# The convolution of a batch in other chunks between the pieces of a large matmul, and one copy moved ahead of the next stage

## Chip, cores, metric

One core of a Trainium2 chip (trn2). The metric is the device time of one execution in microseconds (us). Every run quoted gave a correct result. The profiled span is some 1.8 us shorter than the device time of the same execution.

## The reference, cut

```
# x: (8, 4224, 192) f32; weight: (8 heads, 7 taps)
w = softmax(weight, axis=-1)                       # per head
x = causal convolution over the sequence, 7 taps, head h on its 24 channels
h = x^T @ U @ V                                    # U (4224, 32), V (32, 4224): mixes the sequence
u = x + h^T
out = u + max(u @ w_ch1, 0) @ w_ch2                # 192 -> 768 -> 192
```

## The kernel before

It works in bf16 with float32 accumulation. A *group* is 8 tiles of 128 sequence positions, 33 groups in all. W1 is the product with `w_ch1` and its relu, W2 that with `w_ch2`. A late *stage* `k` does W1 of three groups and then twelve pieces of W2 (12 matmuls each); between the pieces it does the work that later stages need: the convolution of batch `k-2` (`c`), the collection `y^T U` (`t`), its sum (`s`), and the low-rank product and addition (`h`). The number ahead of the colon is the piece ahead of which it is done.

```
elif k < 10:                      # stages of batches 4 to 7 (k = 6 to 9)
    b = k - 2
    at = {
        1: [f"c{b}:0:3:AAD"],     # first head : heads : engines that evict (A ScalarE, D VectorE)
        2: [f"c{b}:3:3:AAD"],
        3: [f"c{b}:6:2:A"] + ([f"x{b + 1}:3"] if b + 1 < B else []),
        5: [f"t{b}", hs[0]],
        7: [f"s{b}"],
        8: [hs[1]],
        11: [hs[2]],
    }
```

Matmuls write into eight *banks* of PSUM, taken in rotation. An *eviction* is the operation by which ScalarE or VectorE brings a result out of its bank; only when it is over can the bank be taken again.

The convolution reads x and a copy of it shifted across partitions, `xb`. GpSimd makes that copy in six steps. `x5:3` runs three of them at that place in the program; the others follow one by one behind the loads of the next x, which matmuls of the next W1 let go:

```
def conv32(b, h0, nh, engs):
    ...
    for n in range(nh):
        pp = [bank(), bank()]                     # 8 PSUM banks, in rotation
        for cg in range(4):                       # 64x32 tiles: x and xb by turns
            ...
        for part in range(2):
            evac(engs[(2 * n + part) % len(engs)], yt[b][...], pp[part][...])
...
for g in gs1:
    ends = w1(g, ...)
    for b, blocks in LOADS.items():
        for q, (gb, m) in enumerate(blocks):
            if gb == g:
                x_load(b, q, ends[m])             # held back until that matmul of W1
                if steps:
                    steps.pop(0)()                # one copy of xb
```

`xb` has one buffer, so the copies for the next batch can start only when the convolution of this one is over. The evictions of W1 are alternately ScalarE's and VectorE's (seven and five of twelve a group).

## Time and profile before

| | before |
|---|---|
| three runs ahead of the prediction, median (range) | 325.4 us (325.24 to 325.87) |
| profiled span | 323.5 us |
| TensorE busy, granted clock | 317.1 us (98%), 1.00 |
| VectorE, ScalarE, GpSimd busy | 269.1, 170.4, 142.7 us |
| W1 to next W1, stages of batches 4 to 7 | 28.04, 28.28, 28.13, 28.12 us (112.57 in all) |
| W1's end to the collection, in each of them | 7.19 to 7.20 us |

The last two rows are differences of start times in the chain of the work that ended last, whose columns are start (us), length (us), engine, tile, line and number of instructions. L554 is W1, L583 W2, L339 the convolution, L402 the collection, L428 the sum, L457 the low-rank product.

### The profile page before, as it was taken

The page shows a single profiled execution, that of the slowest core. Times are in us where ns is not written, and L with a number is a line of the kernel's source. Part 1 is how long each engine was busy: PE and PEld are TensorE (multiplying, and loading weights), DVE is VectorE, ACT ScalarE, POOL GpSimd, SP SyncE. Part 2 cuts the span into 40 slices and gives each one's busy share as a digit, 9 for nine tenths or more (in the row PEclk, how much of TensorE's full clock was granted, in tenths as well). Part 3 has the DMA queues.
Part 4 walks back from the last instruction along what each step waited for, and adds up shares of the span by engine and source line. Part 5 has one row for each costly group of instructions (what it writes and reads, how often), then busy time and mean ns, then how long its engine had stood idle before and what let it go on. Part 6 is the DMA issues. An engine that isn't in the chain of part 4 may idle for free.

```text
span 323.5 us, 9584 instructions
## 1 busy us (share of the span) xinstructions
PE 317.1 (98%) x3996; PEld 223.2 (69%) x3996; DVE 269.1 (83%) x551; ACT 170.4 (53%) x344; POOL 142.7 (44%) x111
## 2 busy tenths in 40 slices
PE   6999999999999999999999999999999999999996
PEld 3757676478677647866864784587797497487495
DVE  6769989987977986998798699879898897896864
ACT  1766624860874397088339708824903902912920
POOL 8664179729947694786859497000000000000000
PEclk9999999999999999999999999999999999999999
DMA  8999993999996899699699976139269059048035
GB/s 104 192 192 178 209 211 99 203 195 248 210 153 180 229 175 169 170 162 195 166 238 183 192 162 181 33 112 244 58 168 267 8 149 268 25 121 271 2 119 176
DMA packets 122907, 53.52 MB, mean 165 GB/s; under 512 B 87760, under 2 KB 122832, under 8 KB 122864
## 3 DMA queue, kind: packets, MB, share of 16 engines
q1 hardware_dynamic: 84528, 38.08, 47.0%
q0 software_dynamic: 38192, 14.73, 39.6%
q8 instruction: 31, 0.51, 0.7%
q14 instruction: 12, 0.10, 0.1%
q10 hardware_dynamic: 144, 0.10, 0.1%
HBM read 29.49 MB, written 25.95 MB: 171 GB/s over the span
## 4 chain that ended last, share of the span: by engine, by line
PE 92%; ACT 3%; DMA 2%; DVE 1%; issue 0%; POOL 0%; POOLq 0%
PE ps L583 42%; PE ps L554 39%; PE ps L339 3%; PE ps L457 3%; DMA x_sb<-in_x_dram 2%; PE ps L402 2%; ACT rl_sb L568 2%; PE ps L369 1%; ACT y_sb L256 1%; PE ps L509 1%; DVE u_sb L479 1%; DVE rl_sb L570 1%; PE ps L524 0%; PE ps L428 0%; POOL x_sb L79 0%
## 5 line engine op out<-in xcount | busy, mean ns | idle before, releaser
L568 ACT ACTIVATE rl_sb<-ps 128x512 bf16<-128x512 f32 x233 | 124.3, 603 | 108.0 <-PE ps L554 96.0
L583 PE MATMUL ps<-W_sb,rl_sb 128*128 128x192 bf16 x1584 | 141.9, 246 | 0.2
L583 PEld LDWEIGHTS <-rl_sb 128*128 128x128 bf16 x1584 | 128.1, 98 | 13.5 <-issue 13.1
L554 PE MATMUL ps<-uT,W_sb 64*128 64x512 bf16 x1188 | 131.7, 376 | 0.0
L570 DVE TENSOR_SCALAR rl_sb<-ps 128x512 bf16<-128x512 f32 x163 | 105.3, 688 | 15.7 <-PE ps L554 15.4
L554 PEld LDWEIGHTS <-W_sb 64*128 64x128 bf16 x1188 | 66.9, 94 | 60.5 <-issue 3.9
L592 DVE TENSOR_TENSOR out_sb<-ps,u_sb 128x384 f32<-128x384 f32 (+1 forms) x133 | 70.4, 550 | 25.9 <-PE ps L583 25.4
L305 POOL COPY xb_sb<-x_sb 32x3072 bf16<-32x3072 bf16 (+1 forms) x24 | 67.6, 2826 | 0.7
L479 DVE TENSOR_TENSOR u_sb<-y_sb,ps 128x192 bf16<-128x192 bf16 (+1 forms) x168 | 66.3, 461 | 0.0
L293 POOL COPY xb_sb<-x_sb 128x3072 bf16<-128x3072 bf16 x12 | 32.6, 2744 | 34.6 <-PE ps L339 25.7
L256 ACT ACTIVATE y_sb<-ps 128x384 bf16<-128x384 f32 (+4 forms) x90 | 38.2, 514 | 10.7 <-PE ps L339 7.9
L79 POOL DMA_DIRECT2D x_sb<-in_x_dram x32 | 27.1, 849 | 17.5 <-PE ps L554 10.5
L258 DVE CAST y_sb<-ps 128x408 bf16<-128x408 f32 (+4 forms) x36 | 19.2, 578 | 1.1 <-PE ps L369 0.9
L457 PE MATMUL ps<-tt_sb,V_sb 32*128 32x192 bf16 x264 | 12.4, 246 | 0.1
L339 PE MATMUL ps<-xb_sb,band 64*32 64x384 bf16 x192 | 12.1, 332 | 0.0
L339 PE MATMUL ps<-x_sb,band 64*32 64x384 bf16 x192 | 12.1, 333 | 0.0
L457 PEld LDWEIGHTS <-V_sb 32*128 32x128 bf16 x264 | 4.7, 92 | 7.3 <-issue 7.3
L416 ACT ACTIVATE tt_hi<-ps 128x192 bf16<-128x192 f32 x8 | 2.6, 331 | 10.9 <-PE ps L402 10.9
L369 PE MATMUL ps<-x_sb,band 64*64 64x240 bf16 (+3 forms) x192 | 8.1, 276 | 0.3 <-DMA x_sb<-in_x_dram 0.3
L369 PEld LDWEIGHTS <-band 64*64 64x64 bf16 x192 | 6.0, 106 | 2.2 <-issue 1.5
L339 PEld LDWEIGHTS <-band 64*32 64x32 bf16 x384 | 4.5, 89 | 4.1 <-issue 3.0
L402 PE MATMUL ps<-y_sb,U_sb 128*32 128x192 bf16 x258 | 7.4, 247 | 0.0
(65 smaller groups left out, 69.0 us busy)
## 6 DMA issues: line engine op xcount, KB each, us to landing
out_dram<-out_sb SPq DMA_DIRECT2D x131, 192.0 KB, 2.7
x_sb<-in_x_dram POOLq DMA_DIRECT2D x14, 384.0 KB, 7.3
x_sb<-in_x_dram POOLq DMA_DIRECT2D x7, 432.0 KB, 7.3
x_sb<-in_x_dram POOLq DMA_DIRECT2D x7, 408.0 KB, 8.0
x_sb<-in_x_dram POOLq DMA_DIRECT2D x1, 504.0 KB, 7.6
uT<-u_sb SPq DMA_TRANSPOSE x31, 3.9
x_sb<-in_x_dram POOLq DMA_DIRECT2D x1, 480.0 KB, 5.9
W_sb<-in_moe_w_ch_dram POOLq DMA_DIRECT2D x2, 192.0 KB, 7.6
```

The costliest lines, as they stand in the source:

```text
L79: return nc.gpsimd.dma_start(out=xt[b][HB * r : HB * r + HB, s0:s1, :], in_=x[b, blk * HB : (blk + s1 - s0) * HB, :].rearrange("(j p) d -> ...
L256: nc.scalar.activation(out=out, in_=in_, func=ACT.Copy)
L293: nc.gpsimd.tensor_copy(out=xbt[b][:, s0:s1, :], in_=xt[b][:, s0 + 1 : s1 + 1, :])
L305: nc.gpsimd.tensor_copy(out=xbt[b][q, s0:s1, :], in_=xt[b][q, s0:s1, :])
L339: nc.tensor.matmul(out=pp[r][QB * cg : QB * cg + QB, 0 : nk[r] * GS], lhsT=w[hr], rhs=t[hr, st : st + 2 * nk[r] - 1 : 2, hs], start=True, ...
L457: nc.tensor.matmul(out=banks[pr][:, a * D : (a + 1) * D], lhsT=V_sb[32 * q : 32 * q + 32, (j // 8) * 2 + j % 2, :], rhs=ttb[b][32 * q : 32 ...
L479: nc.vector.tensor_tensor(out=u_group(g)[:, i : i + n, :, hf, :], in0=yt[b][:, run[0] : run[0] + n, :].rearrange("p n (c k) -> p n c k", c=3),
L554: last = nc.tensor.matmul(out=pps[m][hf][:], lhsT=W1_sb[HB * hf : HB * hf + HB, c, m * P : (m + 1) * P], rhs=uTt[g][HB * hf : HB * hf + HB ...
L568: nc.scalar.activation(out=rl[:, m, hf, :], in_=pp[hf][:], func=ACT.Relu)
L570: nc.vector.tensor_scalar_max(out=rl[:, m, hf, :], in0=pp[hf][:], scalar1=0.0)
L583: last = nc.tensor.matmul(out=cps[:, a * D : (a + 1) * D], lhsT=rlt[g][:, m, hf, (i + a) * P : (i + a + 1) * P], rhs=W2_sb[:, m, :], start ...
L592: nc.vector.tensor_tensor(out=o[:, 0:n, :].rearrange("p n (c k) -> p n c k", c=3), in0=cps[:, 0 : n * D].rearrange("p (n c k) -> p n c k", ...
```

## The change

Its intent: begin the convolution right behind W1, in chunks of 2, 3 and 3 heads instead of 3, 3 and 2 behind the first three pieces; and have GpSimd do four instead of three of its six copies before the next W1, so that they are over when the earlier chunk needs them.

```diff
@@ stage of batch 3
-                4: ["c3:6:2:A", "x4:3"],
+                4: ["c3:6:2:A", "x4:4"],
@@ stages of batches 4 to 7
-                1: [f"c{b}:0:3:AAD"],
-                2: [f"c{b}:3:3:AAD"],
-                3: [f"c{b}:6:2:A"] + ([f"x{b + 1}:3"] if b + 1 < B else []),
+                0: [f"c{b}:0:2:A"],
+                2: [f"c{b}:2:3:AAD"],
+                3: [f"c{b}:5:3:AAD"] + ([f"x{b + 1}:4"] if b + 1 < B else []),
```

## The prediction

> **What bounds the kernel now.** I read the page first (shares of the engines, granted clock), then the chain of work that ended last, then the timeline of one late stage on ScalarE, TensorE and GpSimd, then the groups by form in a stretch with GpSimd copies and one without.
>
> The page's first and second part:
>
> ```profile
> PE 317.1 (98%) x3996; PEld 223.2 (69%) x3996; DVE 269.1 (83%) x551; ACT 170.4 (53%) x344; POOL 142.7 (44%) x111
> PEclk9999999999999999999999999999999999999999
> ```
>
> TensorE is busy for 317.1 of 323.5 us at full clock. Of the 6.4 us left, little lies in the stages that the change touches. A late stage (batches 3 to 7, about 28.1 us each) is W1 of three groups (108 matmuls, L554), then twelve pieces of W2 (12 matmuls each, L583), with the convolution of one batch (L339) put between the first pieces, then the collection (L402), the sum and the low-rank products (L457). The change touches the four stages of batches 4 to 7. The chain in the first of them (start, length, what):
>
> ```profile
> 109.54 11.76 PE ps L554 x108
> 121.30 1.10 PE ps L583 x12
> 122.40 0.64 PE ps L339 x19
> 123.04 1.10 PE ps L583 x12
> 124.13 0.71 PE ps L339 x17
> 124.84 1.10 PE ps L583 x12
> 125.94 0.47 PE ps L339 x11
> 126.41 2.09 PE ps L583 x24
> 128.49 0.85 PE ps L402 x33
> ```
>
> There is no other engine and no wait in these stages: the chain is TensorE alone, end to end. The kernel is bound by TensorE's own work, so a change of order can gain only what the order itself costs. Three sizes come out of these rows. A W2 run of 12 takes 1.10 and one of 24 takes 2.09, so 12 matmuls more cost 0.99 (82.5 ns each) and each run has a fixed part of 1.10 - 0.99 = 0.11 us. A convolution run of three heads takes 0.64, of two heads 0.47, so 0.17 a head and a fixed 0.13 us. The second run of three heads takes 0.71 where the first takes 0.64, so 0.07 us is a small wait. It is the same in the other three stages (0.71 each time).
>
> The ScalarE and TensorE timeline of the same stage shows who is near to holding TensorE up:
>
> ```profile
> 120.36 1.58 ACT L568 ACTIVATE rl_sb<-ps 128x512 bf16<-128x512 f32 x3
> 122.75 5.22 ACT L256 ACTIVATE y_sb<-ps 128x384 bf16<-128x384 f32 x12 [0.81 <-PE ps L339]
> 129.38 0.33 ACT L416 ACTIVATE tt_hi<-ps 128x192 bf16<-128x192 f32 x1 [1.41 <-PE ps L402]
> 124.48 0.34 PE L339 MATMUL ps<-x_sb,band 64*32 64x384 bf16 x2
> ```
>
> ScalarE's last relu of W1 ends at 121.94, only 0.64 us after W1, so it carries no backlog out of W1. Its twelve evictions of the convolution run at 5.22 / 12 = 0.435 us each and end at 127.97, 0.5 us before the collection at 128.49, which needs all of them. The fourth ends near 122.75 + 4 x 0.435 = 124.49, just when the third head of the second run goes on (124.48): that is the wait of 0.07 us.
>
> GpSimd, from the end of one W1 to the next:
>
> ```profile
> 118.58 3.08 POOL L305 COPY xb_sb<-x_sb 32x3456 bf16<-32x3456 bf16 x1
> 121.59 0.88 POOL L79 DMA_DIRECT2D x_sb<-in_x_dram  x1
> 126.55 5.43 POOL L293 COPY xb_sb<-x_sb 128x3072 bf16<-128x3072 bf16 x2 [4.08 <-PE ps L339]
> 132.58 2.74 POOL L305 COPY xb_sb<-x_sb 32x3072 bf16<-32x3072 bf16 x1
> 135.38 0.17 POOL L74 MEMSET x_sb<- 64x96 uint32 x1
> 138.67 0.82 POOL L79 DMA_DIRECT2D x_sb<-in_x_dram  x1 [3.12 <-PE ps L554]
> ```
>
> The last shifted copy of x for this batch ends at 121.66. The convolution starts at 122.40, so it has 0.7 us to spare; right behind W1 (121.30) it would come too late by 0.4 us. After three copies (to 135.32) GpSimd is idle until 138.67, when the first load of the next x is let go by W1.
>
> **What the Trainium skill says.** "TensorEngine Tiling (Array Packing)", Key Properties, says that a change of tiling mode, not merely of tile, drains TensorE. This kernel uses 64x128 tiles in W1, 128x128 in W2 and 64x32 in the convolution. The fixed 0.11 and 0.13 us of a run agree with it, though the trace does not show the drain itself. "TensorE: Matmul & The Clock Gate", Part 1, gives columns / 2.4 GHz + about 2.5 ns per warm matmul: 192 columns make 82.5 ns, which is just what the rows above give. So the W2 work itself cannot shrink. "Perfetto Trace Analysis", Identifying the Most-Contended Engine, warns that matmul busy time does not tell how near the roof a kernel is; that is why I go by the lengths of runs and not by the 98%. "SBUF — State Buffer", Terms, says that VectorE and GpSimd contend for a shared pair of ports, the loser blocking fully. If that bit here, moving a copy would move VectorE's time. It does not: the relu takes VectorE 690 ns in a stage with copies and 686 in one without.
>
> ```profile
> L570 DVE TENSOR_SCALAR rl_sb<-ps 128x512 bf16<-128x512 f32 x15 | 9.8, 690 | 1.2 <-PE ps L554 1.2
> L570 DVE TENSOR_SCALAR rl_sb<-ps 128x512 bf16<-128x512 f32 x15 | 9.5, 686 | 1.2 <-PE ps L554 1.2
> ```
>
> **The change part by part.** The counts stay: 64 matmuls of convolution, 144 of W2, 12 ScalarE and 4 VectorE evictions, six copies per batch. Only the order changes.
>
> 1. Chunks. Before, behind W1: W2 12, three heads, W2 12, three heads, W2 12, two heads, W2 24, collection. After: two heads, W2 24, three heads, W2 12, three heads, W2 24, collection. The convolution still makes three runs, W2 three instead of four. One fixed part of 0.11 us falls away. By the rows: before 1.10 + 0.64 + 1.10 + 0.71 + 1.10 + 0.47 + 2.09 = 7.21 (the chain has 128.49 - 121.30 = 7.19). After, with the 0.07 kept: 0.47 + 2.09 + 0.64 + 1.10 + 0.71 + 2.09 = 7.10. Gain 0.11 us a stage, four stages: 0.44 us. This takes a step from W1 to the convolution to cost as much as one from W1 to W2, which no row of before shows.
>
> 2. Banks (eight in rotation). With time 0 at W1's end: the first two heads take the banks of the third and fourth relu pair of the last group, free by then. Their four evictions follow the last relu at 0.64 and end at 0.64 + 4 x 0.435 = 2.4. The first three-head run starts at 2.56 and its third head, at 2.9, needs the last of those: 0.5 us to spare. The second three-head run starts at 4.30; its third head, at 4.64, needs the bank of ScalarE's eighth eviction. That run of evictions begins about 0.42 after its heads (as 122.75 stands to 122.33, the start of the first convolution matmul), at 2.98, and its fourth ends at 2.98 + 4 x 0.435 = 4.72. So a wait of some 0.08 us, as before: the pattern is the same.
>
> 3. Collection. ScalarE's last four evictions begin near 4.72 and end near 6.5; the collection starts at 7.10. 0.6 us to spare, so no new wait.
>
> 4. Fourth copy. The convolution ends at 5.01 instead of 5.11, so copies start at about 126.45; three end at 135.2, the fourth (2.74) at 138.0 and the memset at 138.2, still ahead of the load's release near 138.6. Nothing is held up. In W1 two copies remain: 138.6 + 0.85 + 2.7 + 0.85 + 3.05 = 146.1, against 149.7 before (146.61 + 3.08 there). W1 ends at about 149.3, so the first chunk has 3 us to spare. In the first of the stages the three copies end at about 108.3 and the fourth at 111.1; the load comes 0.4 us later than its 110.64, and the last copy near 118.6, against 121.2 needed. So the fourth copy pays for the earlier chunk and does nothing by itself.
>
> Sum: 325.4 - 0.44 = 325.0 us.
>
> **The rivals.** (a) The early chunk waits for a bank or for ScalarE's relu tail. For it: ScalarE is at work until 0.64 us past W1. Against it: the rotation gives the first four banks to relus that ended a microsecond or more before. If every stage lost 0.3 us, the time would be 325.4 - 0.4 + 1.2 = 326.2. (b) The copies come too late for the early chunk. For it: only 0.7 us were to spare. Against it: step 4. If the fourth copy hit the load's release, the wait would be up to 0.4 us a stage: 326.6. (c) The step from W1 to the convolution, both with 64 rows, costs less than that from W1 to W2, or the 0.07 vanishes as well: 0.1 to 0.2 us a stage more, 324.4. (d) The intent could be a larger gain by easing ScalarE or VectorE. Against it: the chain names neither in these stages, so nothing of theirs can come back.
>
> **Range and chances.** The three runs of before lie between 325.24 and 325.87, which is as wide as the gain. (c) sets the lower end, 324.4; a part of (a) or (b) the upper, 325.8. Being 2% faster would need 6.5 us, 1.6 a stage, in stages whose chain is all TensorE work: 0.005. Being 2% slower would need a stall of over 1.6 us in each of four stages: 0.01. Within 2%: 0.985.
>
> **What would show it.** In the chain of the changed kernel: W1, then a convolution run near 0.47, W2 24 near 2.09, runs of 0.64 and near 0.71, and 7.10 from W1's end to the collection; stages shorter by 0.1 us, all before and behind them unchanged. GpSimd's last copy ends 3 us ahead of W1's end and its idle time before the load nearly vanishes. I would be wrong where a convolution row exceeds these lengths by 0.2 us or more, where the chain names ScalarE or GpSimd behind W1, or where W1 itself lengthens.

## The result, and the profile after

| | before | after |
|---|---|---|
| median of 6 runs (range) | 325.25 us (325.08 to 325.87) | 325.0 us (324.94 to 325.84) |
| ratio, 95% interval | | 0.9995 (0.9983 to 1.0008) |
| profiled span | 323.5 us | 323.2 us |
| W1 to next W1, four stages | 112.57 us | 112.15 us |
| W1's end to the collection | 7.19 to 7.20 us | 7.09 us |
| TensorE busy | 317.1 us | 317.6 us |

A ratio is the mean time of one kernel's fast runs over that of the other's fast runs of the same rounds, so it is not quite the ratio of the medians. By time alone the two kernels cannot be told apart: the interval holds 1. The stages tell them apart, because the same row repeats in all four to about 0.01 us. The gain lasts to the end of the chain: VectorE's last addition starts at 319.82 instead of 320.32. Of these 0.50 us, 0.42 are of the four stages, and 0.08 were there ahead of them (109.46 against 109.54).

The chain of the changed kernel in the first of these stages (columns as above); the last two lines are of the sum and the W2 run behind it:

```profile
109.46 11.76 PE ps L554 x108
121.22 0.47 PE ps L339 x11
121.69 2.09 PE ps L583 x24
123.78 0.64 PE ps L339 x19
124.42 1.10 PE ps L583 x12
125.52 0.71 PE ps L339 x17
126.22 2.09 PE ps L583 x24
128.31 0.85 PE ps L402 x33
...
131.52 0.17 PE ps L428 x2
131.69 0.99 PE ps L583 x12
```

Before, there were W2 runs of 12, 12, 12 and 24 matmuls from W1's end to the collection; now there are 24, 12 and 24. The collection stands at 128.31 - 121.22 = 7.09 us instead of 7.19. Nothing else moved: W1 is 11.76 as before (11.92 in the second of these stages, before and after), and the rows behind the collection are the same. The last line matters for the reason: the sum uses a full 128x128 tile as W2 does, and the W2 run behind it takes 0.99, not the 1.10 that a run of 12 takes behind a convolution.

The timeline of ScalarE and TensorE in that stage (columns: start, length, engine, line, operation, out<-in, count, and idle time ahead with what ended it):

```profile
121.75 1.69 ACT L256 ACTIVATE y_sb<-ps 128x384 bf16<-128x384 f32 x4
124.13 3.42 ACT L256 ACTIVATE y_sb<-ps 128x384 bf16<-128x384 f32 x8 [0.69 <-PE ps L339]
125.86 0.35 PE L339 MATMUL ps<-x_sb,band 64*32 64x384 bf16 x2
```

ScalarE takes the first chunk's four evictions without a pause and is done at 123.44, 0.3 us before the next chunk; the second lot of eight ends at 127.55, 0.8 us before the collection. The fourth of that lot is done near 124.13 + 4 x 3.42 / 8 = 125.84, and TensorE goes on at 125.86: the small wait of before is still there.

GpSimd of the changed kernel over the same stretch:

```profile
115.35 3.08 POOL L305 COPY xb_sb<-x_sb 32x3456 bf16<-32x3456 bf16 x1
...
132.38 5.43 POOL L305 COPY xb_sb<-x_sb 32x3072 bf16<-32x3072 bf16 x2
137.87 0.17 POOL L74 MEMSET x_sb<- 64x96 uint32 x1
138.49 0.82 POOL L79 DMA_DIRECT2D x_sb<-in_x_dram  x1 [0.45 <-PE ps L554]
```

The last copy for this batch ends at 118.43, 2.8 us ahead of W1's end, where it had ended 0.4 us behind it. The fourth copy fits into what was idle time: GpSimd now waits 0.45 us for the load's release, where it waited 3.12. At the start of the first of these stages there is less room: no wait is left, and the load is issued at 111.00 instead of 110.64.

### The profile page after: what moved, and what is told of

It reads as the page before. It is cut to its first block, busy times and chain, and to the rows that moved or that the text cites. A ratio compares the mean times of both kernels' runs of the same rounds, so it can differ in the third digit from the quotient of the medians.

```text
span 323.2 us, 9583 instructions
## 1 busy us (share of the span) xinstructions
PE 317.6 (98%) x3996; PEld 223.7 (69%) x3996; DVE 268.6 (83%) x551; ACT 170.0 (53%) x344; POOL 142.7 (44%) x111
## 4 chain that ended last, share of the span: by engine, by line
PE 92%; ACT 3%; DMA 2%; DVE 1%; issue 0%; POOL 0%; POOLq 0%
PE ps L583 42%; PE ps L554 39%; PE ps L339 3%; PE ps L457 3%; DMA x_sb<-in_x_dram 2%; PE ps L402 2%; ACT rl_sb L568 2%; PE ps L369 1%; ACT y_sb L256 1%; PE ps L509 1%; DVE u_sb L479 1%; DVE rl_sb L570 1%; PE ps L524 0%; PE ps L428 0%; POOL x_sb L79 0%
## 5 line engine op out<-in xcount | busy, mean ns | idle before, releaser
L153 PE MATMUL ps<-zz 128*128 128x512 f32 (+1 forms) x10 | 6.7, 816 | 1.1 <-DVE zz L143 1.1
```

## The experiments

Eight kernels. All outputs are right. Against noise, all are read first by the time from the W1 of the first changed stage to the W1 behind the fourth:

| run | four stages, us | against the changed kernel | expected | median time, us | profiled span, us |
|---|---|---|---|---|---|
| before | 112.57 | +0.42 | | 325.48 and 325.29 (11 runs each) | 323.5 |
| after | 112.15 | | | 325.0 | 323.2 |
| order_only | 113.43 | +1.28 | +1.3 | 326.22 | 324.4 |
| copy_only | 112.57 | +0.42 | +0.4 | 325.28 | 323.4 |
| twos | 112.80 | +0.65 | +0.72 | 325.46 | 325.9 |
| engs | 111.87 | -0.28 | -0.28 | 324.77 | 323.4 |
| three_first | 112.20 | +0.05 | -0.28 | 324.98 | 323.1 |
| fours | 113.16 | +1.01 | +0.8 | 326.06 | 324.5 |
| six_ahead | 112.15 | 0.00 | 0 | 325.06 (one run) | 323.3 |
| five_stages | 111.87 | -0.28 | -0.28 | 324.64 | 323.0 |

One run each of order_only (332.46) and three_first (330.46) was slow; neither counts in a ratio, and the medians move by no more than 0.01 us without them.

The theory: TensorE's own work bounds these stages, each run of another kind costs it a fixed 0.11 to 0.13 us, and waits come only where a bank or a copy is late by the rotation and the rows. Its rivals: the early chunk is held up by banks; the copies' timing gains by itself; smaller chunks help by easing ScalarE.

### order_only: the fourth copy undone

```diff
-                4: ["c3:6:2:A", "x4:4"],
+                4: ["c3:6:2:A", "x4:3"],
-                3: [f"c{b}:5:3:AAD"] + ([f"x{b + 1}:4"] if b + 1 < B else []),
+                3: [f"c{b}:5:3:AAD"] + ([f"x{b + 1}:3"] if b + 1 < B else []),
```

> The new chunks with only three copies ahead (the second part of the change undone). Theory (the fourth copy is there to pay for the early chunk): the last shifted copy ends some 0.2 to 0.4 us after W1 in the stages of batches 4, 5 and 6, as it did before, and the first convolution matmul, ready at W1's end, waits for it: 0.3 to 0.5 us in each of three stages, none in that of batch 7 (no loads hold its copies up). From the start of the first convolution run to the collection about 7.09 as in the changed kernel, but W1's end to there 7.4 to 7.6. Profiled span 323.2 + 1.3 = 324.5, time about 326.3. Rival (the copies had room enough, the fourth does nothing): span 323.2, time 325.0.

The chain now leaves TensorE and runs over GpSimd in the first and the third stage (the first is shown), and the wait view of TensorE has one line for it:

```profile
118.44 3.09 POOL xb_sb L305
121.58 0.54 PE ps L339 x10
122.11 2.09 PE ps L583 x24
```

```profile
PE ps L339 <- POOL xb_sb L305: 0.3, 2, 0.2
```

The copy ends behind W1's end (109.40 + 11.76 = 121.16), and W2 starts at 122.11, 0.95 us after W1's end instead of 0.47. The four stages lose 0.48, 0.31, 0.49 and 0.00 us, 1.28 in all; the fourth has no loads that hold its copies. This settles that the early chunk needs the fourth copy. The chunks alone would have made the kernel slower than before: 326.22 against 325.48, ratio 1.0019 (1.0003 to 1.0035).

There is a lesson in the wait view: it shows 0.3 us, and 1.28 us were lost. The first convolution matmul that reads x's copy started, its end is modelled a third of a microsecond later, and the wait of the next one shows only where it outlasts that end. Lengths of runs in the chain showed all of it.

### copy_only: the chunks undone

```diff
-                0: [f"c{b}:0:2:A"],
-                2: [f"c{b}:2:3:AAD"],
-                3: [f"c{b}:5:3:AAD"] + ([f"x{b + 1}:4"] if b + 1 < B else []),
+                1: [f"c{b}:0:3:AAD"],
+                2: [f"c{b}:3:3:AAD"],
+                3: [f"c{b}:6:2:A"] + ([f"x{b + 1}:4"] if b + 1 < B else []),
```

> The old chunks (3, 3, 2 heads behind the first, second and third W2 piece) with four copies ahead. Theory: the copies were off the path already, so nothing changes: from W1 to the collection 7.19 as before, span 323.5, time 325.25 as the kernel before; the last copy ends some 3 us before W1 does. Rival (the earlier copy itself gains, by taking GpSimd out of W1's stretch): stages shorter by 0.1 us and W1 shorter than 11.76, span 323.2.

The four stages take 112.57 us, the same as before to the hundredth, with the same runs (1.10, 0.64, 1.10, 0.71, 1.10, 0.47, 2.09). The fourth copy does nothing by itself.

### twos: one more run of each kind

```diff
-                2: [f"c{b}:2:3:AAD"],
-                3: [f"c{b}:5:3:AAD"] + ([f"x{b + 1}:4"] if b + 1 < B else []),
+                1: [f"c{b}:2:2:AAD"],
+                2: [f"c{b}:4:2:AAD"],
+                3: [f"c{b}:6:2:ADD"] + ([f"x{b + 1}:4"] if b + 1 < B else []),
```

> The convolution in four chunks of two heads, right behind W1 and behind the first three W2 pieces: a run of convolution and a run of W2 more than in the changed kernel, same matmuls. Theory (each run costs a fixed 0.11 to 0.13 us on TensorE): four convolution runs of 0.47 and W2 runs of 1.10, 1.10, 1.10 and 2.09, so 4 x 0.47 + 3 x 1.10 + 2.09 = 7.27 from W1 to the collection against 7.09, with the 0.07 wait gone; 0.18 a stage, 0.72 in four; span 323.9, time 325.7. Rival (what counts is that evictions are spread, smaller chunks ease ScalarE): the stage gets shorter or stays, span 323.2 or less.

W1's end to the collection is 130.71 - 123.45 = 7.26 us (7.27 expected), with runs of 0.47, 1.10, 0.47, 1.09, 0.47, 1.10, 0.47 and 2.08. More switches cost more, by the size read off the profile of before, and spreading the evictions gains nothing that makes up for it.

The profiled run was 2 us longer than expected (325.9 against 323.9) for a reason that lies ahead of the changed stages. Its chain there runs over one output transfer:

```profile
71.45 8.61 DMA out_dram<-out_sb
```

Such a transfer lands after 2.7 us in the median. VectorE waited 2.4 us for it, and the next W1 ended 2.2 us later than in the changed kernel. Code that all the kernels share did this, so the span of this run is not held against the chunks.

### engs: the engines of two evictions exchanged

```diff
-                2: [f"c{b}:2:3:AAD"],
+                2: [f"c{b}:2:3:AADADA"],
```

> The changed kernel with one eviction of the middle chunk moved from ScalarE to VectorE (fourth eviction of the chunk's pattern: the fifth head's first half). Theory (the third head of the last chunk waits 0.07 us for the bank that this ScalarE eviction frees last): the run of 0.71 becomes 0.64, W1's end to collection 7.03 instead of 7.09, 0.07 x 4 = 0.28 us less in all; span 322.9, time 324.7. Rival (the third run is long for another reason, tiles or VectorE): it stays at 0.71, span 323.2; or VectorE gets in the way and a later row grows.

The letters are dealt to the chunk's evictions in turn, so the edit does a little more than this says: the fifth eviction goes from ScalarE to VectorE, and the sixth from VectorE to ScalarE in exchange. ScalarE keeps four of the six.

```profile
124.86 1.10 PE ps L583 x12
125.96 0.64 PE ps L339 x19
```

The last chunk takes 0.64 instead of 0.71 in all four stages. The bank named in the prediction is shown to be the cause of the 0.07: with VectorE doing that eviction the wait is gone. The bank of the sixth goes to the W2 run behind the last chunk, which still takes 2.09. The profiled span (323.4) does not show it, as this run began the changed stages 0.45 us later than the changed kernel's; the stages do.

### three_first: three heads right behind W1 (a miss)

```diff
-                0: [f"c{b}:0:2:A"],
-                2: [f"c{b}:2:3:AAD"],
-                3: [f"c{b}:5:3:AAD"] + ...
+                0: [f"c{b}:0:3:AAD"],
+                2: [f"c{b}:3:3:AAD"],
+                3: [f"c{b}:6:2:A"] + ...
```

> The changed kernel with the chunks 3, 3, 2 instead of 2, 3, 3 at the same places (behind W1, the second and the third W2 piece). Theory (banks by rotation): the third head behind W1 takes the banks of the last group's fifth relu pair, free 0.1 us after W1, so it does not wait; the second chunk comes when all evictions of the first are over, and the last has only two heads, so the wait of 0.07 is gone: runs of 0.64, 2.09, 0.64, 1.10, 0.47, 2.09, together 7.03 against 7.09, 0.07 x 4 less, span 322.9. Rival (the chunk behind W1 was made small because ScalarE's relu tail holds it up): the first run is longer than 0.7 and the sum over 7.1.

```profile
119.35 2.55 ACT rl_sb L568 x5
121.90 0.04 issue
121.94 2.14 PE ps L583 x24
```

The expected 7.03 became 128.37 - (109.48 + 11.76) = 7.13. The later runs are as expected (0.64, 1.10, 0.47), so the 0.07 is gone. The heads themselves did not wait, but the first W2 piece did, in three of the four stages: by the rotation it takes the bank of the last relu that ScalarE evicts, free at 121.89 (the timeline has six relus from 118.69 for 3.20). I had checked the banks of the heads and not that of the piece behind them. With two heads first, the first piece takes a bank freed earlier. The second stage confirms it: W1 is 0.15 us longer there, ScalarE's last relu ends 0.49 us behind it instead of 0.65, and the piece does not wait: the collection comes at 156.40 - 149.38 = 7.02, as expected. So the first chunk is near its limit: two heads fit ahead of the relu tail (the relus that still run when W1 is over), and three cost 0.1 us where the tail is the longer one.

### fours: two chunks of four heads

```diff
-                0: [f"c{b}:0:2:A"],
-                2: [f"c{b}:2:3:AAD"],
-                3: [f"c{b}:5:3:AAD"] + ...
+                0: [f"c{b}:0:4:AAD"],
+                3: [f"c{b}:4:4:AAD"] + ...
```

> Two chunks of four heads, behind W1 and behind the third W2 piece: one run of convolution less than in the changed kernel, the W2 runs as many. If only the number of runs counted, 0.13 us a stage less: 6.96 from W1 to the collection, span 322.7. Theory with banks: the fourth head behind W1 takes the banks of the last relu pair, which ScalarE and VectorE free 0.64 and 0.76 us after W1 where TensorE is there at 0.44, and the last head of the second chunk waits for the output of the piece ahead of it; so first run about 1.1, W2 3.08, second about 1.0, W2 2.09: 7.3 in all, 0.2 a stage more than the changed kernel, span 324.0; more if ScalarE's last evictions come late for the collection.

```profile
119.80 2.55 ACT rl_sb L568 x5
122.36 0.04 issue
122.40 0.48 PE ps L339 x6
122.88 3.08 PE ps L583 x36
125.96 1.01 PE ps L339 x25
```

W1 ends at 121.70, so the first chunk takes 1.18 (1.1 expected) and the second 1.01 (1.0 expected), 7.35 to the collection. The chain passes through ScalarE's relu, as said. The last head of the second chunk goes on at 126.61, just behind VectorE's addition for the piece ahead of it, which ends at 125.99 + 0.56 = 126.55. Fewer runs are better only as far as the banks go: the fixed 0.13 saved is less than the waits for banks.

### six_ahead: all copies ahead of W1 (one look)

```diff
-  "x4:4"  and  f"x{b + 1}:4"
+  "x4:6"  and  f"x{b + 1}:6"
```

> All six copies of x ahead of the next W1 instead of four. Theory (the copies need only be over by W1's end, and the loads only land before the next copies): the last copy ends some 5 us before W1's end, the first load is issued some 5 us later than in the changed kernel (near 144 instead of 138.5), all stages keep their lengths, W1's end to the collection 7.09, span 323.2. Rival (GpSimd's work in W1's stretch, or the time of the loads, touches the stage): W1 or the stage changes by 0.1 us or more, or the copies of the next stage wait for the loads.

```profile
116.76 3.35 POOL L79 DMA_DIRECT2D x_sb<-in_x_dram  x4
...
129.58 2.74 POOL L293 COPY xb_sb<-x_sb 128x3072 bf16<-128x3072 bf16 x1 [0.41 <-DMA x_sb<-in_x_dram]
```

The loads come 5.8 us later than in the changed kernel (111.00 there), and in this stage one copy waits 0.41 us for them, but no stage changes. The number of copies ahead has a floor (four) and room above it.

### five_stages: what the experiments point to

The changed kernel with the exchange of engs, and the stage of batch 3 in the same order:

```diff
-                2: ["c3:0:3:AAD"],
-                3: ["c3:3:3:AAD"],
-                4: ["c3:6:2:A", "x4:4"],
-                5: [hs[0]],
-                6: ["t3"],
-                8: ["s3", hs[1]],
+                0: ["c3:0:2:A"],
+                2: ["c3:2:3:AADADA"],
+                3: ["c3:5:3:AAD", "x4:4"],
+                5: ["t3", hs[0]],
+                7: ["s3"],
+                8: [hs[1]],
```

> A version meant to beat both: the changed kernel with the eviction moved as in engs and with the same order also in the stage of batch 3 (2, 3, 3 heads; collection and sum at the places of the later stages). Theory by counting runs: in that stage two W2 runs fewer (0.22) and no wait (0.07), so W1 to next W1 28.30 becomes 28.01; with 0.07 x 4 of engs, 0.57 us less than the changed kernel: span 322.6, time 324.4. The copies of batch 3 end 1.5 us before W1's end, so no wait there. Rival: the earlier stage has less to spare (its inputs come late), and a wait shows behind its W1.

```profile
81.55 11.83 PE ps L554 x108
...
109.57 11.76 PE ps L554 x108
```

That stage takes 28.02 us (28.01 expected, 28.30 in the changed kernel), the four others 111.87. The expected 0.22 us of W2 came about differently than counted: W2 has one run fewer (seven, not eight), and one of the seven now stands behind the sum, where it has no fixed part. The time is 324.64 us against 325.29 for the kernel before in the same rounds, ratio 0.9975 (0.9960 to 0.9990). It is the only kernel whose interval lies below 1. The span was 323.0 where 322.6 was expected, because the first of these stages began at 81.55 instead of 81.16.

## Why the prediction was right, point by point

- **TensorE bounds the stages:** shown. The rows of the chain after are TensorE's alone, and all that was gained is TensorE's.
- **Step 1, a W2 run less, 0.11 us a stage:** shown. 7.09 instead of 7.19; four stages 112.15 instead of 112.57, so 0.42 where 0.44 was predicted. The one thing that no row of before had shown, the step from W1 to the convolution, costs as much as supposed: the run takes 0.47 as it does behind W2. Rival (c) falls.
- **Step 2, banks:** shown. No run of convolution is longer than named, the 0.07 stays at the third chunk's last head, and engs shows that its cause is the named bank. Rival (a) falls for two heads; three_first and fours show that it begins with three and four. The reason given against it was too good, though: the relus that free the first four banks ended 1.3, 0.8, 0.5 and 0.3 us ahead of W1's end, not all of them "a microsecond or more" before.
- **Step 3, collection:** shown, with 0.8 us to spare instead of the 0.6 worked out.
- **Step 4, the fourth copy:** shown on both sides. copy_only gains nothing, order_only loses 1.28 us. GpSimd still waits 0.45 us for the load's release, and where it does not (the first stage) the last copy is still 2.8 us early, so rival (b) falls. In the first stage the last copy ends at 118.43 (118.6 predicted).
- **The sum:** 325.0 predicted, 325.0 measured. That the two agree to the tenth is partly luck: medians of before moved between 325.25 and 325.48 from one set of runs to the next, and by the medians of the six runs the gain is 0.25 us and not 0.44. The stages are the proof, not the median.
- **VectorE beside GpSimd's copies:** not tested. The relu that the prediction compares (690 and 686 ns) takes its input from PSUM, so it says nothing of VectorE operations that read SBUF. The result does not rest on it: copy_only shows that the moved copy changes no stage.

What stays open: that the fixed part of a run is the change of the tile's shape is supported by the W2 run behind the sum (same shape, no fixed part) and by its appearing at every other change, but no run separated a drain of the array from other fixed costs of a switch. Why W1 takes 11.91 or 11.92 us in the second of these stages, in every run, was not looked into.

## What to carry to other kernels

Where the chain of a stage is one engine's own work, read its fixed cost per run of equal instructions off rows of different lengths, and count runs before and after a reordering: that gives the gain to a hundredth of a microsecond. Then check each early arrival against the buffers it takes, including that of the first instruction behind the moved block, and against the slowest producer of its inputs; a reordering that gains 0.1 us can lose 0.5 by one late copy. Where a gain is as small as the spread of runs, compare the repeating stage rather than the whole time.

## What the Trainium skill lacked or had wrong

- "TensorEngine Tiling (Array Packing)", Key Properties, says that a change of tiling mode drains TensorE, and gives no size there. Here a run cost a fixed 0.11 us (W2, 128x128: 1.10 for 12 matmuls and 2.09 for 24) or 0.13 us (convolution, 64x32), and a W2 run behind a matmul of the same shape had no fixed part (0.99 for 12).
- "Perfetto Trace Analysis", Per-instruction lifecycle, says that a matmul's reported end is estimated. What follows for reading waits is missing: in order_only the wait view showed 0.3 us of 1.28 us lost, as most of the wait lay under the modelled end of the matmul ahead.
- No page that I read tells how far single transfers of one kind scatter: one output transfer was 8.61 us in the chain, where the median to landing is 2.7 us, and the next W1 ended 2.2 us later for it.
